# Quarter products with w_in one block earlier, with three moves in the order of the work: a recurrent attention block and an MLP on one Trainium2 core

## The chip, the core and the metric

The kernel runs on one core of a Trainium2 chip. A core has five engines that work through queues of their own and wait for one another by semaphores: TensorE (PE, with its weight loads shown apart as PEld), VectorE (DVE), ScalarE (ACT), GpSimd (POOL) and SyncE (SP), which here only issues DMA transfers. The metric is the time of one execution in microseconds, taken as the median of several.

## The reference

The inputs are q, k, v of 4 batches, 8 heads, 768 time steps and 48 numbers, a beta per step, and two weight matrices. A delta rule runs over time, with a 48 × 48 state per batch and head, and an MLP with a hard-swish follows on its 3072 × 384 output:

```python
for t in range(S):
    kt, vt, bt = k_n[:, :, t], v[:, :, t], beta[:, :, t, None]   # k_n: k over its norm
    y[:, :, t] = einsum('bhd,bhde->bhe', q[:, :, t], state)
    v_old = einsum('bhde,bhd->bhe', state, kt)
    state = state + bt[..., None] * einsum('bhd,bhe->bhde', kt, vt - v_old)
x = y as (3072, 384)
h = x @ w_in                                   # 384 x 2048
out = (h * clip(h + 3, 0, 6) / 6) @ w_out      # 2048 x 384
```

## The kernel before

**Steps and groups.** Time is cut into N = 24 token steps of 32 time steps, each for all four batches at once (4 × 32 = 128 rows). Within a step the recurrence is solved with an inverse of a unit triangular 32 × 32 matrix per head. A step has two halves: `prep(t)`, some steps ahead, which normalizes the keys (kb, L510, on POOL), transposes keys and queries (pt, L524), copies them out of PSUM (KQ, L532, on ACT), forms the scores (sc, L547, 32 small products) and masks them into L and LB (L558, on DVE); and `chain(t)`, which needs the state: products with the state (ks, L806), the right side R (L901, L909, on DVE), its product with the inverse (pz, L827), the update of the state (su, L938; L956), the output (py, L827; y, L819 and L863) and its transposition (yt, L873) into xT (L877). Four steps make a group, whose inverses DVE forms together in some 60 small instructions (L759, L764) between two transpositions (L469, L473). The norms of a group's keys are squares (L409, on POOL), row sums (L413, on DVE) and a few small instructions.

**Blocks of the MLP.** Two steps make one of 12 blocks of 256 tokens. Each block has an up stage (x times w_in, then hard-swish into g) and a down stage (g times w_out). Up comes in two forms. `up` takes sixteen units, each three products of 128 × 256, a relu on ACT (L1001) and a product on DVE (L1004). `up_by_eleven` treats two of the three slices of w_in as 2 × 2 quarters and takes seven products of 128 × 128 and two of 128 × 256 for a pair of units instead of six of 128 × 256. It needs the sums S1, S2, S4 and W21 of quarters of w_in (`weight_sums`, 16 instructions on POOL, L1030) and, for each block, four sums of the tokens (`token_sums`, L1056, on DVE). In it, `begin(j)` issues four products and copies them out (L1080 on ACT, two additions L1030 on POOL); `end(j)` issues the other five and adds (L1093, L1097 on DVE); then come `first` (L1100 and the relu L1104, on ACT) and `rest` (L1107, on DVE). The relu writes into a buffer of the pool name "o", of which there is one, the same in which the down stage's result lies until it is stored. The down stage is `down_by_seven` from block 2 on: 7 products of quarters in 14 units, with additions on DVE and POOL (L1228), copies on ACT (L1225) and, at the end, eight stores (L1143) issued by SP, in the last block by SP and ACT.

**The order.** Everything is issued in an order written by hand; each engine works through its part of it in order. Up to step 4 a list of words (`ORDER`) sets it. From step 5 on a loop does it: each step t has 15 units u; in each unit a table `plan` issues a piece of the chain or of `prep` of a later step, then one unit of the MLP follows, then some instructions of the inverse or the norms (`fill`), as many as a budget (`USED`, `CHAIN`, `mode`) allows. The MLP's unit stands behind the chain's piece in each unit, so products of both alternate on PE. Two steps are 30 units, and a block is 14 + 16 units, so each block meets the same pieces of the chain. Up of block b begins in unit 12 of step 2b + 1, and its remaining units fall to step 2b + 2.

**PSUM.** Two rings of buffers: "pm", four tiles, for most products, and "pc", two tiles of two banks, for ks, sc and su. A product waits until the tile that it takes has been read.

These lines say where the forms change and where the scores of a step are issued:

```python
UF = 5                                    # blocks from UF on: up_by_eleven
...
sums = weight_sums() if blk == UF - 1 else iter(())
...
2: lambda: (take(ch), take(now), take(gens["q"], 4)),   # queries transposed
3: lambda: take(ch),
4: lambda: (take(ch), take(now)),         # chain: pz; prep: scores
5: lambda: take(now),                     # prep: L and LB, then bkb
6: lambda: take(now),
8: lambda: take(ch),                      # chain: su and py
```

Of the kernel before, what the change touches and what calls it, by code (L numbers as in the profile page):

```python
# [44 lines left out]
def kernel(  # L45
# [23 lines left out]
    DM, FF = moe_w_in.shape  # L69
    C, DP = 32, 64  # L70
    P = B * C
    assert P == 128 and S % C == 0 and D <= DP and H % 2 == 0
    N = S // C
# [6 lines left out]
    CB = 2  # L80
# [14 lines left out]
    def rows(b):  # L95
        return slice(C * b, C * b + C)
# [59 lines left out]
    def read(*keys):  # L156
        for key in keys:
            past.add(("read", key))
            reads.setdefault(key, len(reads))
# [53 lines left out]
    for j, value in enumerate((1.0, -1.0)):  # L213
        m = mask2[:, j, :]
        for b in range(B):
            nc.gpsimd.memset(mask2[rows(b), j, :], value)
            nc.gpsimd.affine_select(
                out=mask2[rows(b), j, :], in_=mask2[rows(b), j, :], pattern=[[1, C]],
# [796 lines left out]
                past.add(("up", blk))  # L1015
            yield

    UF = 5
    S1, S2, S4 = (sums_in[:, i] for i in range(3))

    def w_tiles(s, i):
# [37 lines left out]
    def up_by_eleven(blk):  # L1059
        needs(("sums", blk))  # L1060
        B11, T3x, B21, B22, _, _ = x_tiles(blk)
        B3 = xTs[blk][:, 2].rearrange("p (i c) -> p i c", c=P)
        phs, ready = {}, {}

        def mm(ph, n, w, x, start=False, stop=False):
            nc.tensor.matmul(  # L1066
                ph[:, n], lhsT=w, rhs=x, start=start, stop=stop, skip_group_check=True
            )

        def begin(j):  # L1070
            key = ("ph", blk, "by", j)
            ring("pm", NPM, key)
            ph = phs[j] = psM.tile([128, 4, P], FP32, name="ph", tag=slot["pm"])
            mm(ph, 0, W11[:, j], B11, start=True)
            mm(ph, 1, S1[:, j], T1x)
            mm(ph, 2, W21[:, j], T3x)
            mm(ph, 3, S2[:, j], T2x)
            gs[blk, j] = g_all[:, 2 * j : 2 * j + 2]
            gt = gs[blk, j].rearrange("p i (t c) -> p (i t) c", c=P)
            nc.scalar.activation(out=gt, in_=ph[:], func=ACTF.Copy)  # L1080
            plus_minus(gt[:, 3:1:-1], gt[:, 0:2], gt[:, 3:1:-1], ALU.add)
            plus_minus(gt[:, 0], gt[:, 0], gt[:, 2], ALU.add)

        def end(j):
            ph = phs.pop(j)
            mm(ph, 0, W12[:, j], B21)
            mm(ph, 1, S4[:, j], B22)
            mm(ph, 2, W22[:, j], T4x)
            mm(ph, slice(0, 2), W13[:, j], B3)
            mm(ph, slice(2, 4), W23[:, j], B3, stop=True)  # L1090
            g = gs[blk, j].rearrange("p i c -> p (i c)")
            gt = gs[blk, j].rearrange("p i (t c) -> p (i t) c", c=P)
            nc.vector.tensor_tensor(  # L1093
                out=gt[:, 1:3], in0=ph[:, 1:3],
                in1=gt[:, 3].unsqueeze(1).to_broadcast([128, 2, P]), op=ALU.add,
            )
            nc.vector.tensor_tensor(out=gt[:, 3], in0=ph[:, 3], in1=gt[:, 0], op=ALU.add)  # L1097

            def first():
                nc.scalar.activation(out=gt[:, 0], in_=ph[:, 0], func=ACTF.Copy)  # L1100
                read(("ph", blk, "by", j))
                ro = mlp.tile([128, CB, DM], FP32, name="o", bufs=1)
                r = ro[:].rearrange("p c m -> p (c m)")[:, 0 : 2 * TB]
                nc.scalar.activation(out=r, in_=g, func=ACTF.Relu, bias=half, scale=1.0 / 6.0)  # L1104

                def rest():
                    nc.vector.scalar_tensor_tensor(  # L1107
                        out=g, in0=r, scalar=1.0, in1=g, op0=ALU.min, op1=ALU.mult
                    )

                ready[j] = rest

            ready[j] = first
            if j == NPR - 1:
                past.add(("up", blk))

        def go(j):
            if j in ready:
                ready.pop(j)()

        begin(0)
        yield
        begin(1)
        yield
        for j in range(NPR):
            end(j)
            go(j - 1)
            if j + 2 < NPR:
                yield
                begin(j + 2)  # L1130
                go(j)
                yield
            else:
                go(j)
                if j == NPR - 1:
                    go(j)
                yield

    def to_dram(t, o):
        for b in range(B):  # L1140
            r0 = b * S + t * C
            eng = nc.scalar if t >= N - CB and b % 2 else nc.sync
            eng.dma_start(out=out[r0 : r0 + C, :], in_=o[rows(b ^ 1)])  # L1143

    def down(blk, c, f0):

# [32 lines left out]
    HF, HM = NFC // 2, DM // 2  # L1179
# [19 lines left out]
    def down_by_seven(blk):  # L1199
        def A(f, i, j, n=2):  # L1200
            return g_all[:, f + HF * j : f + HF * j + n, i * P : i * P + P]

        def sums(op, out, a, b, f):
            nc.vector.tensor_tensor(out=A(f, *out, 4), in0=A(f, *a, 4), in1=A(f, *b, 4), op=op)  # L1204

        lo, hi, A11, A12, A21, A22 = 0, 4, (0, 0), (0, 1), (1, 0), (1, 1)
        o = mlp.tile([128, CB, DM], FP32, name="o", bufs=1)
        u = mlp.tile([128, HM], FP32, name="u", bufs=1)[:]
        C11, C12, C21, C22 = (o[:, c, m : m + HM] for c in range(CB) for m in (0, HM))
        ps = {}  # L1210

        def product(n, a, b, half):

            if half == 0:
                ring("pm", NPM, ("po", blk, "by", n))
                ps[n] = psM.tile([128, HM], FP32, name="po", tag=slot["pm"])
            for f in range(half * HF // 2, (half + 1) * HF // 2):
                nc.tensor.matmul(  # L1218
                    ps[n][:], lhsT=A(f - f % 2, *a)[:, f % 2], rhs=b[:, f],
                    start=(f == 0), stop=(f == HF - 1),  # L1220
                )

        def copy(out, n, scale=1.0):
            read(("po", blk, "by", n))
            nc.scalar.activation(out=out, in_=ps[n][:], func=ACTF.Copy, scale=scale)  # L1225

        def add(out, a, b, eng=nc.vector):
            eng.tensor_tensor(out=out, in0=a, in1=b, op=ALU.add)  # L1228

        near = nc.gpsimd if blk + 1 < N // CB else nc.vector  # L1230

        settle()
        product(1, A11, B11, 0)
        yield
        product(1, A11, B11, 1)
        copy(u, 1)
        yield
        product(4, A22, T4, 0)
        yield
        product(4, A22, T4, 1)  # L1240
        copy(C21, 4, -1.0)
        sums(ALU.add, A22, A21, A22, lo)
        yield
        product(2, A12, B21, 0)
        sums(ALU.add, A22, A21, A22, hi)
        yield
        product(2, A12, B21, 1)
        copy(C11, 2)
        sums(ALU.subtract, A21, A11, A21, lo)
        yield  # L1250
        product(5, A22, T1, 0)
        sums(ALU.subtract, A21, A11, A21, hi)
        yield
        product(5, A22, T1, 1)
        copy(C22, 5)
        add(C11, C11, u, near)
        sums(ALU.subtract, A11, A22, A11, lo)
        yield
        product(7, A21, B12, 0)
        sums(ALU.subtract, A11, A22, A11, hi)  # L1260
        yield
        product(7, A21, B12, 1)
        copy(C12, 7)
        sums(ALU.subtract, A12, A12, A11, lo)
        yield
        product(6, A11, T2, 0)
        sums(ALU.subtract, A12, A12, A11, hi)
        yield
        product(6, A11, T2, 1)
        yield  # L1270
        product(3, A12, B22, 0)
        add(u, u, ps[6][:])
        read(("po", blk, "by", 6))
        add(C12, C12, u, near)
        add(C21, C21, C12, near)
        yield
        add(u, u, C22, near)
        add(C22, C22, C12, near)
        to_dram(blk * CB + 1, o[:, 1])
        product(3, A12, B22, 1)  # L1280
        add(C12, u, ps[3][:])
        read(("po", blk, "by", 3))
        to_dram(blk * CB, o[:, 0])
        yield

    def mlp_units():
# [43 lines left out]
    def take(gen, n=1):  # L1330
        for _ in range(n):
            while next(gen, None) == 1:
                pass
# [107 lines left out]
    with tc.manual_schedule():  # L1441
# [11 lines left out]
        loads = iter(())  # L1453
        left = due = 0
        USED = {"up": 0.42, "eleven": 1.0, "down": 0.7}
        CHAIN = {0: 0.45, 1: 0.75, 2: 0.75, 3: 0.4, 4: 0.4, 6: 0.5, 9: 0.8, 10: 0.6, 14: 0.2}
        for t in range(LS, N):
            g, i = group(t)
            ch = chain_of(t)
# [8 lines left out]
            if i == 2:  # L1468
# [3 lines left out]
                1: lambda: (take(ch), take(now)),  # L1472
                2: lambda: (take(ch), take(now), take(gens["q"], 4)),
                3: lambda: take(ch),
                4: lambda: (take(ch), take(now)),
                5: lambda: take(now),
                6: lambda: take(now),
                8: lambda: take(ch),
                9: lambda: take(ch),
                10: lambda: take(ch),  # L1480
# [70 lines left out]
```

## Time and profile before

| | |
|---|---|
| median of 3 runs | 666.08 us (665.9 to 666.21) |
| the profiled execution | 669.68 us, its span from first to last instruction 667.9 us |
| granted TensorE clock, mean | 0.98 |
| SP's and ACT's transfers, share of 16 DMA engines' span | 21.1% and 0.2% |

The profile comes from one execution. Its page lists the busy time of each engine, the chain of work that ended last, and groups of like instructions by source line; the trace behind it answers questions on windows, lines and waits. A row of the timeline begins with start and duration in us; behind it, in brackets, stands the time that the engine sat idle before and what ended that. In the chain, "issue" is time in which an engine waited for nothing that the profile shows. PE's records come two for each product of the source, and each has a weight load beside it in PEld.

### The profile page before, as it was taken

The numbers are of one execution on the slowest core, as the hardware profiler recorded it, in microseconds if no ns is written. First come the engines' busy times: TensorE is split into PE (matmuls) and PEld (weight loads), VectorE is DVE, ScalarE is ACT, GpSimd is POOL, SyncE is SP. The second block draws the span as 40 slices with busy tenths as digits, with TensorE's granted clock in tenths as the row PEclk, the third lists the DMA queues.
The fourth block names the chain that finished last, engine by engine and source line by source line (L and its number), as shares of the span: only waits on it lengthen the run. The fifth ranks groups of instructions, "written<-read, shape, count | busy, mean of one in ns | idle before, by whom it ended". The sixth has DMA issues, their size and how long they took to land.

```text
span 667.9 us, 26330 instructions
## 1 busy us (share of the span) xinstructions
PE 636.2 (95%) x11544; PEld 568.0 (85%) x11544; DVE 485.9 (73%) x1146; ACT 272.6 (41%) x532; POOL 203.9 (31%) x320
## 2 busy tenths in 40 slices
PE   2658999999999999999999999999999999999997
PEld 2547987776689988988989989999999999999997
DVE  5879876899545697747988857988748988456353
ACT  5887779432133132232244244245244144153250
POOL 6421032002511130463155255055052241331430
PEclk9767999999999999999999999999999999999999
DMA  7996247302040030031030030020020020010000
GB/s 175 223 240 157 71 97 168 61 13 49 18 89 14 3 73 2 2 79 32 3 68 9 2 67 10 2 62 2 3 50 2 2 49 2 20 21 2 25 1 25
DMA packets 88499, 33.27 MB, mean 50 GB/s; under 512 B 80160, under 2 KB 83232, under 8 KB 88384
## 3 DMA queue, kind: packets, MB, share of 16 engines
q1 hardware_dynamic: 88128, 31.29, 21.1%
q8 instruction: 91, 1.49, 0.9%
q10 hardware_dynamic: 256, 0.30, 0.2%
q14 instruction: 24, 0.20, 0.1%
HBM read 26.84 MB, written 4.72 MB: 47 GB/s over the span
## 4 chain that ended last, share of the span: by engine, by line
PE 88%; DVE 3%; ACT 3%; DMA 2%; issue 2%; SPq 1%; POOL 0%; ACTq 0%; DVEq 0%; POOLq 0%
PE po L1218 28%; PE ph L1066 20%; PE ph L994 15%; PE po L1154 6%; PE ks L806 3%; PE su L938 3%; PE pt L524 3%; PE pz L827 3%; PE py L827 3%; PE sc L547 2%; DMA kf<-in_k_dram 2%; ACT spare L356 2%; PE yt L873 1%; PE pi L684 1%; DVE pr L730 0%
## 5 line engine op out<-in xcount | busy, mean ns | idle before, releaser
L1066 PE MATMUL ph<-xT,w_in 128*128 128x128 f32 (+1 forms) x560 | 121.6, 321 | 0.7 <-issue 0.4
L994 PE MATMUL ph<-xT,w_in 128*128 128x256 f32 (+1 forms) x576 | 117.6, 354 | 1.0 <-ACT xT L877 0.6
L1218 PE MATMUL po<-w_out,g 128*128 128x192 f32 x640 | 110.6, 326 | 0.0
L994 PEld LDWEIGHTS ph<-xT,w_in 128*128 128x128 f32 x576 | 95.6, 195 | 13.8 <-ACT xT L877 1.0
L1218 PEld LDWEIGHTS po<-w_out,g 128*128 128x128 f32 x640 | 104.6, 190 | 0.5
L1066 PEld LDWEIGHTS ph<-xT,w_in 128*128 128x128 f32 x560 | 91.1, 191 | 6.0 <-ACT KQ L532 0.7
L1030 POOL TENSOR_TENSOR g<-g 128x256 f32<-128x256 f32 x112 | 68.0, 609 | 83.4 <-ACT g L1080 79.0
L1218 PE MATMUL po<-spare,g 128*128 128x192 f32 x480 | 86.7, 332 | 0.0
L1218 PEld LDWEIGHTS po<-spare,g 128*128 128x128 f32 x480 | 77.2, 190 | 1.8
L1001 ACT ACTIVATE g<-ph,halves 128x256 f32<-128x256 f32 (+1 forms) x96 | 41.2, 436 | 75.7 <-PE ph L994 75.7
L1228 POOL TENSOR_TENSOR o<-o,u 128x192 f32<-128x192 f32 x18 | 13.2, 733 | 175.7 <-ACT o L1225 97.2
L1080 ACT ACTIVATE g<-ph 128x512 f32<-128x512 f32 x56 | 33.4, 597 | 81.3 <-PE ph L1066 81.3
L1204 DVE TENSOR_TENSOR g<-g 128x512 f32<-128x512 f32 x80 | 55.6, 716 | 5.6 <-PE po L1218 5.6
L759 DVE TENSOR_TENSOR pr<-A 128x30 f32<-128x30 f32 (+9 forms) x150 | 56.8, 379 | 2.7
L764 DVE TENSOR_TENSOR A<-A,pr 128x30 f32<-128x30 f32 (+9 forms) x150 | 55.7, 371 | 3.7
L1004 DVE SCALAR_TENSOR_TENSOR g<-g,ph 128x256 f32<-128x256 f32 (+1 forms) x96 | 34.7, 371 | 29.4 <-ACT g L1001 29.2
L356 ACT ACTIVATE spare<-spare,places 128x768 uint16<-128x768 uint16 (+1 forms) x56 | 52.5, 942 | 2.8 <-DMA kf<-in_k_dram 1.7
L1093 DVE TENSOR_TENSOR g<-ph,g 128x256 f32<-128x256 f32 x56 | 23.5, 420 | 38.5 <-PE ph L1066 33.8
L1225 ACT ACTIVATE o<-po 128x192 f32<-128x192 f32 x40 | 13.2, 330 | 83.2 <-PE po L1218 79.6
L1107 DVE SCALAR_TENSOR_TENSOR g<-o,g 128x512 f32<-128x512 f32 x56 | 40.7, 726 | 6.0 <-ACT o L1104 5.9
L1154 PE MATMUL po<-w_out,g 128*128 128x384 f32 x128 | 45.0, 489 | 0.0
L1104 ACT ACTIVATE o<-g,halves 128x512 f32<-128x512 f32 x56 | 40.5, 722 | 10.1 <-DVE g L1107 5.7
(141 smaller groups left out, 988.1 us busy)
## 6 DMA issues: line engine op xcount, KB each, us to landing
kf<-in_k_dram SPq DMA_DIRECT2D x96, 48.0 KB, 2.9
qb<-in_q_dram SPq DMA_DIRECT2D x96, 48.0 KB, 2.6
vf<-in_v_dram SPq DMA_DIRECT2D x96, 48.0 KB, 2.2
out_dram<-o SPq DMA_DIRECT2D x92, 48.0 KB, 1.6
spare<-in_moe_w_in_dram SPq DMA_DIRECT2D x4, 768.0 KB, 5.8
w_out<-in_moe_w_in_dram SPq DMA_DIRECT2D x4, 768.0 KB, 5.3
w_out<-in_moe_w_out_dram SPq DMA_DIRECT2D x4, 768.0 KB, 6.9
spare<-in_moe_w_out_dram SPq DMA_DIRECT2D x4, 768.0 KB, 5.3
```

The costliest lines, as they stand in the source:

```text
L356: nc.scalar.activation(out=z, in_=z if n else d.bitcast(I16)[:, :, :, 3], func=func, bias=places[:, n : n + 1], scale=scale,)
L759: nc.vector.tensor_tensor(out=pv, in0=A[:, j + 1 :, j].unsqueeze(2).to_broadcast([n, w, j]), in1=A[:, j, 0:j].unsqueeze(1).to_broadcast([n ...
L764: nc.vector.tensor_tensor(out=A[:, j + 1 :, 0:j], in0=A[:, j + 1 :, 0:j], in1=pv, op=ALU.subtract)
L994: nc.tensor.matmul(ph[:, cols], lhsT=w_in[:, s, f * 128 : (f + 1) * 128], rhs=xT[:, s, cols], start=(s == 0), stop=(s == NKT - 1),)
L1001: nc.scalar.activation(out=g, in_=ph, func=ACTF.Relu, bias=half, scale=1.0 / 6.0)
L1030: nc.gpsimd.tensor_tensor(out=out, in0=a, in1=b, op=op)
L1066: nc.tensor.matmul(ph[:, n], lhsT=w, rhs=x, start=start, stop=stop, skip_group_check=True)
L1104: nc.scalar.activation(out=r, in_=g, func=ACTF.Relu, bias=half, scale=1.0 / 6.0)
L1107: nc.vector.scalar_tensor_tensor(out=g, in0=r, scalar=1.0, in1=g, op0=ALU.min, op1=ALU.mult)
L1154: nc.tensor.matmul(pos[c][:], lhsT=gs[blk, f // 2][:, f % 2, c * P : (c + 1) * P], rhs=w_out[:, f, :], start=(f == 0), stop=(f == NFC - 1),)
L1204: nc.vector.tensor_tensor(out=A(f, *out, 4), in0=A(f, *a, 4), in1=A(f, *b, 4), op=op)
L1218: nc.tensor.matmul(ps[n][:], lhsT=A(f - f % 2, *a)[:, f % 2], rhs=b[:, f], start=(f == 0), stop=(f == HF - 1),)
```

## The change

Four edits:

- `UF` is 4 instead of 5: block 4's up is done by `up_by_eleven`, and the sums of w_in's quarters are made during the units of block 3's down stage, not block 4's. The budget of the inverse (`mode`) changes a block earlier with it.
- In `up_by_eleven` of blocks before 9, `first` of pair 0 issues only its copy L1100; the relu follows at the next unit (`second`), and `rest` of pair 0 one unit after that, just ahead of `first` of pair 1.
- For step 12 the scores are issued in unit 6 instead of 4, and L, LB and bkb in unit 7 instead of 5 (`APART`).
- In the last block the first 192 columns of the tile `o[:, 0]` are stored as soon as they are added up, and only the other 192 at the end.

```diff
-    UF = 5
+    UF = 4
...
             def first():
                 nc.scalar.activation(out=gt[:, 0], in_=ph[:, 0], func=ACTF.Copy)
                 read(("ph", blk, "by", j))
+                if j == 0 and blk < 9:
+                    ready[j] = second
+                else:
+                    second()
+
+            def second():
                 ro = mlp.tile([128, CB, DM], FP32, name="o", bufs=1)
                 r = ro[:].rearrange("p c m -> p (c m)")[:, 0 : 2 * TB]
                 nc.scalar.activation(out=r, in_=g, func=ACTF.Relu, bias=half, scale=1.0 / 6.0)
...
                 begin(j + 2)
+                if j == 1:
+                    go(0)
                 go(j)
...
-    def to_dram(t, o):
+    def to_dram(t, o, m=slice(0, DM)):
...
-            eng.dma_start(out=out[r0 : r0 + C, :], in_=o[rows(b ^ 1)])
+            eng.dma_start(out=out[r0 : r0 + C, m], in_=o[rows(b ^ 1), m])
...
         add(C11, C11, u, near)
+        last = blk + 1 == N // CB
+        if last:
+            to_dram(blk * CB, o[:, 0], slice(0, HM))
...
-        to_dram(blk * CB, o[:, 0])
+        to_dram(blk * CB, o[:, 0], slice(HM if last else 0, DM))
...
+        APART = (12,)
...
-                4: lambda: (take(ch), take(now)),
-                5: lambda: take(now),
+                4: lambda: (take(ch), take(now, t not in APART)),
+                5: lambda: take(now, t not in APART),
                 6: lambda: take(now),
+                7: lambda: take(now, t in APART),
```

## The prediction

> **What bounds the kernel now.** I read the page first, then the chain of waits in order of time, then the busy time of the engines block by block. From the page (span, busy times, the queue that brings instructions, the chain by engine):
>
> ```profile
> span 667.9 us, 26330 instructions
> ...
> PE 636.2 (95%) x11544; PEld 568.0 (85%) x11544; DVE 485.9 (73%) x1146; ACT 272.6 (41%) x532; POOL 203.9 (31%) x320
> ...
> q8 instruction: 91, 1.49, 0.9%
> ...
> PE 88%; DVE 3%; ACT 3%; DMA 2%; issue 2%; SPq 1%; POOL 0%; ACTq 0%; DVEq 0%; POOLq 0%
> ```
>
> TensorE is busy for 95% of the span and holds 88% of the chain. The windows below run from one boundary of the chain to the next and hold the up stages of blocks 3, 4, 5, 6 and 7. Columns: us; busy time and instructions of PE, PEld, DVE, ACT, POOL; granted clock; DMA.
>
> ```profile
> 233.76:260.59 26.83, 26.83 (x429) 23.03 (x429) 23.79 (x60) 9.56 (x20) 6.54 (x9) 1.00 0.22 46
> ...
> 284.89:311.72 26.83, 26.83 (x429) 23.04 (x428) 16.36 (x40) 9.56 (x20) 15.46 (x23) 1.00 0.35 69
> ...
> 336.03:362.28 26.25, 25.96 (x478) 23.44 (x477) 22.38 (x52) 12.81 (x26) 14.32 (x23) 1.00 0.23 48
> 386.58:412.90 26.32, 25.90 (x477) 23.59 (x476) 16.26 (x39) 12.93 (x26) 13.52 (x23) 1.00 0.23 48
> 437.21:463.16 25.95, 25.95 (x478) 23.44 (x477) 22.50 (x52) 12.93 (x26) 14.57 (x23) 1.00 0.20 41
> ```
>
> In blocks 3, 4 and 7 PE is as busy as the window is long; what such a stage is worth is PE's own time in it. Blocks 5 and 6 have holes of 0.29 and 0.42 us. The chain shows where they lie:
>
> ```profile
> 311.72 2.60 PE po L1218 x16
> ...
> 339.58 2.80 DMA out_dram<-o
> ...
> 343.02 0.72 ACT o L1104
> 343.74 0.49 ACT KQ L532
> ...
> 344.27 2.69 PE ph L1066 x18
> ...
> 397.14 0.81 PE pz L827 x64
> 397.95 0.79 PE sc L547 x53
> ...
> 399.94 0.42 issue
> ```
>
> In block 5 (from 336.03) the chain leaves PE: the eight stores of block 4's tile land at 342.38, the first relu (L1104) writes the same buffer and starts at 343.02, the copy of the transposed keys (KQ) stands behind it on ACT, and PE's next product waits for the PSUM tile that this copy frees. In block 6 PE stops for 0.42 us with nothing that the profile could name as awaited, just behind pz and sc. So a gain must come from PE's work or from these two holes.
>
> **The change part by part.** The sum is made against the profiled execution, 669.68 us with a span of 667.9; the median of the runs is 666.08, 3.6 us less, and I apply the difference to the median.
>
> 1. Block 4's up by quarter products. Plain up of blocks 3 and 4 takes 26.83 us each, with one token step's chain and one preparation beside it; the quarter products of block 7, with the same chain and preparation (478 − 144 = 334 other instructions against 429 − 96 = 333), take 25.95 without a hole. 26.83 − 25.95 = 0.88 us saved on PE. ACT, DVE and POOL get more to do in this stage: in block 7 DVE was busy 22.50 and POOL 14.57 of 25.95, and PE had no hole, so I take nothing. The four sums of tokens that DVE makes for such a block stand at the end of block 3's down, as block 5's did at the end of block 4's; the chain goes from that down into up on PE. Term: −0.88.
>
> 2. The 16 weight sums on POOL move a block earlier. By the order of instructions, 14 now stand in POOL's queue behind the kb product of 236.97 and run in up of block 3; two follow the addition that opens POOL's tail of the down stage.
>
> ```profile
> 236.36 0.89 DVE L764 TENSOR_TENSOR A<-A,pr 128x210 f32<-128x210 f32 x1
> 237.17 0.41 DVE L1004 SCALAR_TENSOR_TENSOR g<-g,ph 128x256 f32<-128x256 f32 x1
> ...
> 239.27 0.40 DVE L764 TENSOR_TENSOR A<-A,pr 128x228 f32<-128x228 f32 x1
> ...
> 264.22 0.74 DVE L901 SCALAR_TENSOR_TENSOR R<-ks,parity,vf 128x192 f32<-128x192 f32 x2 [0.96 <-PE ks L806]
> 265.80 0.69 DVE L1204 TENSOR_TENSOR g<-g 128x512 f32<-128x512 f32 x1 [0.84 <-PE po L1218]
> ...
> 267.83 1.99 DVE L473 STREAM_TRANSPOSE X<-A 128x1024 f32<-128x1024 f32 x1
> ...
> 236.97 0.96 POOL L510 TENSOR_TENSOR kb<-kf,inv 128x384 f32<-128x384 f32 x1
> ...
> 288.44 0.72 POOL L1030 TENSOR_TENSOR sums_in<-w_in 128x256 f32<-128x256 f32 x1
> ...
> 322.67 1.17 POOL L1030 TENSOR_TENSOR sums_in<-w_in,sums_in 128x256 f32<-128x256 f32 x1
> 323.81 0.86 POOL L1030 TENSOR_TENSOR w_in<-w_in 128x256 f32<-128x256 f32 x1
> ...
> 270.54 0.81 PE pz L827 x64
> ```
>
> Up of block 3 is the stage in which DVE has least room: 23.79 busy of 26.83, since the inverse of a group ends there. The row for two engines at once is L764: 0.89 us with POOL working beside it, 0.40 for a larger tile with POOL idle, so up to 0.49 lost to a POOL instruction; L1004, which reads PSUM, keeps 0.41 under the same POOL instruction. Upper bound 14 × 0.49 = 6.9 us of DVE time, lower bound 0. DVE's room before PE feels it: 26.83 − 23.79 = 3.04 idle, then 0.96 + 0.84 of waits for PE in the down stage, and the transposed inverse is ready at 267.83 + 1.99 = 269.82 for pz at 270.54, another 0.72: 5.56 in all. About half of DVE's instructions there are L759 and L764, so I take some 3.5 us, the middle of the bounds: all inside the room. Term: 0, bounds 0 and +1.3.
>
> The Trainium skill, "GPSIMD Engine Reference", section Specifications, says that POOL shares its SBUF interfaces with VectorE and that they contend when a VectorE instruction has two SBUF inputs. The trace agrees in kind (0.89 against 0.41). Read as full exclusion it is the slower rival below.
>
> 3. The last two sums now stand in front of the squares of the keys (L409), whose sums (L413) DVE awaits in turn.
>
> ```profile
> 271.99 1.27 POOL L409 TENSOR_TENSOR sq<-kf 128x384 f32<-128x384 f32 x1
> ...
> 279.36 0.55 DVE L413 TENSOR_REDUCE ss<-sq 128x8 f32<-128x384 f32 x1 [0.72 <-POOL sq L409]
> 279.83 0.55 DVE L863 TENSOR_TENSOR y<-y,py 128x384 f32<-128x384 f32 x1
> ...
> 281.96 0.33 PE yt L873 x3
> ```
>
> The two took 1.17 + 0.86 = 2.03 us, so the squares, DVE's four L413 and y's addition (L863, ends 280.38) move by up to 2.03, to 282.41. PE takes the transposition of y at 281.96: a wait between 0 and 0.45. DVE was busy when the first square was ready, which swallows part of the shift; I take 0.1. Behind y stand the state update, u's addition and the sums of tokens that open block 4's up; they have the same slack. Term: +0.1.
>
> 4. The relu of a block's first pair, blocks 4 to 8, a unit later. KQ's copy then goes ahead of it on ACT, the stores should have landed by then, and block 5 loses its hole: 26.25 − 25.95 = 0.30; I count the 0.29 of PE. What is late next: relu of the second pair uses the same buffer and waits for DVE's L1107 of the first, which now comes a unit later. Both are 0.7 us pieces (the row 452.78 below is the slow case) on engines that are not full; bounds −0.29 and 0. In block 4 this shift is what covers the stores, which there start as late as in block 5. Term: −0.29.
>
> 5. Step 12's scores (sc, 32 small products) two units later. Instructions reach PE in packets: 2 × 11544 / 91 = 254 each. Counting PE's instructions in both programs, pz of block 6 stands at place 83 of a packet of 256, and there pz and sc, 256 instructions in 1.6 us, were followed by the hole. The quarter products add 100 instructions to block 4, so in block 6 the place becomes 183, which block 3 had before without a hole; place 79 falls to step 12 in block 5, where pz and sc are now parted. So I expect the hole of 0.42 to go: −0.42, bounds −0.42 and 0. The cost: the step issues no DMA, but DVE's L558 and POOL's bkb move with it, past a pair's additions and POOL's two; su needs the PSUM tile that L558 frees.
>
> ```profile
> 449.38 5.05 PE ph L1066 x36
> ...
> 448.96 0.41 DVE L1093 TENSOR_TENSOR g<-ph,g 128x256 f32<-128x256 f32 x1
> ...
> 451.24 0.41 DVE L558 TENSOR_TENSOR LB<-sc,mb 128x256 f32<-128x256 f32 x1
> ...
> 452.78 1.00 DVE L1107 SCALAR_TENSOR_TENSOR g<-o,g 128x512 f32<-128x512 f32 x1
> ```
>
> Before, 36 records (5.05 us) lay between sc and su; now 18, 2.5 us. DVE needs, from a pair's L1093 to the second L558, 451.24 + 0.41 − 448.96 = 2.69 us, and one more inverse instruction (0.4) stands in between; L1093 can start 0.8 us, sc's duration, before sc ends. 3.1 against 3.3: just enough, and L1107 at 1.00 beside POOL takes 0.3 more. Bounds 0 and 0.5; I take 0.15. Terms: −0.42 and +0.15.
>
> 6. The last tile in halves. Four more DMAs, two on SP and two on ACT, are issued in the eighth of the last stage's fourteen units; ACT's next copy comes two units later (16 records, 2.60), and SP has nothing.
>
> ```profile
> 663.33 1.93 ACTq L1143 DMA_DIRECT2D out_dram<-o  x4
> 664.02 0.35 DVE L1228 TENSOR_TENSOR o<-u,po 128x192 f32<-128x192 f32 x1 [0.73 <-PE po L1218]
> ...
> out_dram<-o SPq DMA_DIRECT2D x92, 48.0 KB, 1.6
> ```
>
> At the end the same eight issues remain: four on each queue in 1.93 us, the last of them after DVE's last addition. Only the final four carry half the bytes. A landing of 48 KB takes 1.6 us; if it were all bytes, half of it, 0.8, would go; if it were all latency, nothing. The issues (1.93 for four of 48 KB) are spaced alike whether SP or ACT makes them, so I take the lower end: −0.05, bounds −0.8 and 0.
>
> Sum: −0.88 + 0.1 − 0.29 − 0.42 + 0.15 − 0.05 = −1.39, that is 666.08 − 1.39 = 664.7 us, −0.21%.
>
> **The rivals.**
> - The hole stays, or another packet boundary makes one, so that moving sc gains nothing: −1.39 + 0.42 = −0.97, 665.1. For it: only one hole in the trace to learn from. Against it: of the ten pz directly ahead of sc in blocks 3 to 7, only the one at place 83 had a hole.
> - The relu's shift does nothing, since ACT waits for the stores all the same or for L1107: −1.39 + 0.29 = −1.1, 665.0.
> - The squares come late and PE waits for y: with 0.45 there and as much again at the sums of tokens, −0.6, 665.5.
> - Better than the sum: neither of the two small waits arises and the tail's half lands 0.3 sooner: −1.39 − 0.25 − 0.3 = −1.9, 664.1.
> - The slower one: POOL and DVE exclude each other fully. Then each of the 14 sums costs DVE its 0.72, 10.1 in all, less the room of 5.56: PE waits 4.5 for the inverse or for y, −1.39 + 4.5 = +3.1, 669.2. Against it: DVE read PSUM unhindered under POOL, and waited at most 0.49. The change turns to a loss from (1.39 + 5.56) / 14 = 0.50 per sum, and passes +0.2% at (1.39 + 1.33 + 5.56) / 14 = 0.59.
>
> **How the numbers follow.** 0.2% of 666.08 is 1.33 us, about what a measurement of this kernel can tell from no change. The forecast lies on that bound: its own range, 664.3 to 665.0, is worth 0.45, three quarters of it under 664.75. The better case gets 0.14, the hole 0.14, the relu 0.08, the late squares 0.12, the slower one 0.07. Faster: 0.34 + 0.14 = 0.48; within 0.2%: 0.11 + 0.14 + 0.08 + 0.12 = 0.45; slower 0.07. The range, 663.9 to 665.6, leaves out the slower rival and the ends of the others.
>
> **What would show it.** Right: up of block 4 near 26.0 us with PE busy throughout; no DMA in the chain of block 5; no hole above 0.1 us behind pz; PE without a wait at yt (near 282) and at su of step 12. Wrong: DVE over 26 us busy in up of block 3, PE waiting for L473 or L863 there, KQ's copy still behind L1104, or a hole at another pz. Most likely wrong: PE's waits in the new block 4, for which only blocks 5 to 7 stand as a model.

## The result, and the profile after

The changed kernel takes 664.29 us in the median against 666.21 for the kernel before on the same chip (19 runs each): a ratio of 0.9968, interval 0.9958 to 0.9978, that is 2.1 us less (1.5 to 2.8). The forecast was 664.7, 1.39 us less: the right sign, a time inside the range, and a gain a third too small.

From the page of the changed kernel, span and chain by engine:

```profile
span 660.6 us, 26484 instructions
...
PE 92%; ACT 3%; DVE 2%; DMA 2%; SPq 1%; issue 0%; ACTq 0%; DVEq 0%
```

One execution's span differs from the next by some 5 us, since block 2's up begins anywhere between 175.7 and 180.7 us after the start. Behind it, stages in which PE has no wait, shown or hidden, repeat to 0.03 us. So the runs below are compared stage by stage too. The table is worked out from the traces: us from the first product of a stage to the first of the next, the tail (from the end of DVE's last addition to the end of the span), and the whole from block 2's up to the end of the span. The stages that it leaves out are alike to 0.03 us in all these runs.

```
              before  after    e1     e2     e3     e4     e6     e7     e8     e9    e10
up block 3     26.83  27.09  27.09  26.83  27.10  26.83  28.64  26.83  27.73  26.83  27.10
down block 3   24.31  24.42  24.41  24.31  24.43  24.31  25.37  25.16  29.69  24.31  24.42
up block 4     26.83  25.58  26.08  26.83  25.58  26.83  25.58  25.58  25.58  25.58  25.58
up block 5     26.25  25.78  25.76  25.70  27.18  25.98  25.77  25.77  25.78  25.77  25.78
up block 6     26.32  25.69  25.58  25.58  25.58  26.01  25.68  25.67  25.58  25.68  25.69
down block 6   24.31  24.31  24.38  24.31  24.58  24.31  24.31  24.31  24.31  24.42  24.76
up block 7     25.95  25.85  26.41  25.77  25.92  25.77  25.91  25.81  26.00  25.80  25.94
tail            3.48   3.00   3.39   3.51   2.99   3.02   3.08   2.99   2.99   3.00   2.90
whole         487.22 484.68 486.04 485.78 486.31 486.03 487.29 485.06 490.59 484.35 485.12
```

Between the two profiled executions some 2.5 us went: +0.26 and +0.11 in block 3, −1.25, −0.47, −0.63 and −0.10 in the ups of blocks 4 to 7, −0.48 in the tail. The windows of the same stages in the changed kernel (columns as in the prediction):

```profile
229.02:256.11 27.09, 27.08 (x428) 22.91 (x428) 26.31 (x58) 9.67 (x20) 17.50 (x23) 1.00 0.22 45
256.11:280.54 24.43, 24.43 (x446) 23.19 (x445) 19.18 (x44) 5.09 (x12) 9.57 (x10) 1.00 0.01 3
280.54:306.12 25.58, 25.58 (x477) 23.48 (x477) 16.57 (x40) 12.93 (x26) 14.05 (x24) 1.00 0.37 72
330.43:356.20 25.77, 25.77 (x476) 23.40 (x476) 21.62 (x52) 12.82 (x26) 14.50 (x23) 1.00 0.23 49
```

In up of block 3 POOL is now busy 17.50 instead of 6.54 us and DVE 26.31 instead of 23.79. Block 4 takes 25.58, less than blocks 5 to 7 did before. The chain says why: from the changed kernel, in order of time (start, duration, what).

```profile
251.68 0.55 PE yt L873 x3
...
277.49 0.44 PE yt L873 x3
...
288.49 2.43 PE ph L1066 x18
...
301.83 0.33 PE yt L873 x3
...
340.81 0.81 PE pz L827 x64
341.62 2.62 PE ph L1066 x18
344.25 0.79 PE sc L547 x53
345.04 2.62 PE ph L1066 x18
...
351.91 0.33 PE yt L873 x3
```

The same pieces in the kernel before, in blocks 6 and 7:

```profile
394.54 2.60 PE ph L1066 x18
...
445.17 2.62 PE ph L1066 x18
...
458.69 0.51 PE yt L873 x3
```

The eighteen records ahead of pz take 2.43 us now and took 2.62, 2.60 and 2.69 in blocks 7, 6 and 5. A transposition of y (yt) takes 0.33 when y is there, and 0.51 in block 7 before. So the "busy" PE of block 7, the model for block 4, held 0.19 + 0.18 us of waiting: with the later relu alone (e2) that block takes 0.18 less. In block 3 the same reading shows the price: yt takes 0.55 in up and 0.44 in down, where it took 0.33 before.

### The profile page after: what moved, and what is told of

Read it like the earlier page. It is cut to its first block, busy times and chain, and to the rows that moved or that the text cites. A ratio compares the mean times of both kernels' runs of the same rounds, so it can differ in the third digit from the quotient of the medians.

```text
span 660.6 us, 26484 instructions
## 1 busy us (share of the span) xinstructions
PE 633.3 (96%) x11592; PEld 567.8 (86%) x11592; DVE 492.7 (75%) x1158; ACT 276.7 (42%) x540; POOL 217.0 (33%) x336
## 4 chain that ended last, share of the span: by engine, by line
PE 92%; ACT 3%; DVE 2%; DMA 2%; SPq 1%; issue 0%; ACTq 0%; DVEq 0%
PE po L1226 28%; PE ph L1066 24%; PE ph L994 12%; PE po L1162 6%; PE ks L806 4%; PE pt L524 3%; PE py L827 3%; PE pz L827 3%; PE sc L547 3%; PE su L938 3%; ACT spare L356 2%; DMA kf<-in_k_dram 1%; PE yt L873 1%; PE pi L684 1%; DVE pr L730 1%; DVE A L735 0%
## 5 line engine op out<-in xcount | busy, mean ns | idle before, releaser
L1066 PE MATMUL ph<-xT,w_in 128*128 128x128 f32 (+1 forms) x640 | 139.0, 321 | 0.0
L1066 PEld LDWEIGHTS ph<-xT,w_in 128*128 128x128 f32 x640 | 104.0, 191 | 5.9
L1030 POOL TENSOR_TENSOR g<-g 128x256 f32<-128x256 f32 (+1 forms) x128 | 78.3, 613 | 92.8 <-ACT g L1080 87.8
L994 PE MATMUL ph<-xT,w_in 128*128 128x256 f32 (+1 forms) x480 | 93.3, 343 | 1.5 <-DVE g L1004 1.0
L994 PEld LDWEIGHTS ph<-xT,w_in 128*128 128x128 f32 x480 | 76.2, 190 | 11.5 <-DVE g L1004 1.3
L1080 ACT ACTIVATE g<-ph 128x512 f32<-128x512 f32 x64 | 38.2, 597 | 92.8 <-PE ph L1066 92.8
L759 DVE TENSOR_TENSOR pr<-A 128x30 f32<-128x30 f32 (+9 forms) x150 | 58.8, 392 | 3.1
L764 DVE TENSOR_TENSOR A<-A,pr 128x30 f32<-128x30 f32 (+9 forms) x150 | 56.0, 373 | 3.5
L1001 ACT ACTIVATE g<-ph,halves 128x256 f32<-128x256 f32 (+1 forms) x80 | 33.7, 428 | 56.7 <-PE ph L994 56.7
L1113 DVE SCALAR_TENSOR_TENSOR g<-o,g 128x512 f32<-128x512 f32 x64 | 46.4, 725 | 6.8 <-ACT o L1110 6.8
L1110 ACT ACTIVATE o<-g,halves 128x512 f32<-128x512 f32 x64 | 46.2, 723 | 10.5 <-DVE g L1113 7.8
L1066 PE MATMUL ph<-beta_tok,sums_in 128*128 128x128 f32 x256 | 49.5, 275 | 0.0
L510 POOL TENSOR_TENSOR kb<-kf,inv 128x384 f32<-128x384 f32 x24 | 21.7, 905 | 74.0 <-issue 43.1
```

The lines of the kernel that those rows point to most:

```text
L759: nc.vector.tensor_tensor(out=pv, in0=A[:, j + 1 :, j].unsqueeze(2).to_broadcast([n, w, j]), in1=A[:, j, 0:j].unsqueeze(1).to_broadcast([n ...
L764: nc.vector.tensor_tensor(out=A[:, j + 1 :, 0:j], in0=A[:, j + 1 :, 0:j], in1=pv, op=ALU.subtract)
L994: nc.tensor.matmul(ph[:, cols], lhsT=w_in[:, s, f * 128 : (f + 1) * 128], rhs=xT[:, s, cols], start=(s == 0), stop=(s == NKT - 1),)
L1030: nc.gpsimd.tensor_tensor(out=out, in0=a, in1=b, op=op)
L1066: nc.tensor.matmul(ph[:, n], lhsT=w, rhs=x, start=start, stop=stop, skip_group_check=True)
L1113: nc.vector.scalar_tensor_tensor(out=g, in0=r, scalar=1.0, in1=g, op0=ALU.min, op1=ALU.mult)
```

## The experiments

### The parts alone: e1, e2, e4

**e1: quarter products from block 4, nothing else.**

```diff
-    UF = 5
+    UF = 4
```

> Block 4's up as quarter products alone; the relu, step 12's scores and the tail as before. My theory, after the changed kernel's trace: up of block 3 pays about 0.25 us (y late, 27.1 against 26.83) and its down 0.13 (24.43 against 24.30) for the sums of w_in on POOL; up of block 4 takes 25.6 + 0.2 + 0.3 = 26.1, since its first relu stands behind the stores as block 5's did. The hole of 0.42 leaves block 6; if it hangs on the place of pz and sc in PE's instructions (place 79 of 256 now falls to step 12 of block 5), block 5 gets one of 0.3 to 0.5 behind pz and sc and the sum is -0.3 (665.9 us). Rival: the hole hangs on something else of step 14 (its loads, DVE's order): then it stays in block 6, at 0.4, and block 5 has only its 0.29 at ph. Rival of the prediction for block 4: 25.95 with no wait.

Measured: ratio 1.0006 (0.9986 to 1.0027), no gain; whole 486.04. Block 3 pays the 0.26 and 0.10. Block 4 comes to 26.08, with its first relu behind the stores as foreseen, and block 7, which had no such hole before, gets one:

```profile
PE ph L1066 <- ACT KQ L532: 0.5, 2, 0.2
```

```profile
434.28 2.79 DMA out_dram<-o
...
437.64 0.72 ACT o L1104
438.36 0.49 ACT KQ L532
...
438.90 2.69 PE ph L1066 x18
```

The stores of the block before land at 434.28 + 2.79 = 437.07, L1104 follows, KQ's copy behind it, and PE waits. Block 5, which had this hole in the profile of before, had none here. Which block pays hangs on when the stores land in that execution; the hole is not block 5's own. And block 5 has no stop behind pz and sc, although its instructions stand where I had put the risk: taken alone this speaks against the place.

**e2: the later relu, nothing else** (the `second` of the change's diff, and `go(0)` at j == 1).

> The later relu alone. My theory: it takes KQ's copy from behind L1104 in every block 5 to 7, so up of block 5 goes from 26.25 to 25.77, of block 6 by 0.19 (18 records ahead of pz in 2.43 instead of 2.60), of block 7 by 0.1 to 0.2; block 6 keeps its hole; sum -0.8, 665.4 us. As predicted: only block 5 gains, 0.29, and 6 and 7 nothing. Rival: nothing at all, since ACT waits for the stores anyhow.

Measured: ratio 0.9972 (0.9958 to 0.9987), whole 1.44 us less: −0.55, −0.74 and −0.18 in blocks 5 to 7. Block 6's part holds the 0.42 of its hole, which did not occur in this execution; that is a miss of the expectation, taken up below. Without it 1.02 remains. The relu moves KQ's copy ahead in blocks 5 to 7, not only where a hole was seen, as I had expected after the trace and not in the prediction. By the times this part alone, 0.9972, can't be told from the whole change, 0.9968, while e1 and e4 can't be told from no change.

**e4: the last tile in halves, nothing else** (`to_dram` with `m`, and `last`).

> The last tile in halves alone. Predicted -0.05. From the changed kernel's trace: from the end of DVE's last addition to the end of the span 3.00 us instead of 3.49, so -0.3 to -0.5, 665.8 us, and everything before the last stage as before. Rival: the 0.5 is chance of that one execution, and 3.4 to 3.5 is seen here.

Measured: the tail 3.02, as in the changed kernel (3.00); 48 KB stores gave 3.39 to 3.51 in five traces, 24 KB stores 2.99 to 3.08 in eight. So some 0.4 us is real. The time itself, ratio 1.0001 (0.9985 to 1.0017), can't tell it from nothing. In this execution block 5's first relu waited 0.36 us instead of 0.64, and PE had no hole there. In blocks 6 and 7 KQ's copy was in time without the later relu (2.43 us for the eighteen records), so what the relu saves differs from execution to execution as well. Block 6's stop is there again, 0.28 us long.

### The stop behind pz and sc: e3, e5, e11, e12

**e3: the changed kernel with step 12's scores back in unit 4.**

```diff
-        APART = (12,)
+        APART = ()
```

> The changed kernel with step 12's scores back in unit 4. If the hole hangs on the place in PE's instructions, one of 0.3 to 0.5 us appears in up of block 5 within 2 us behind pz and sc (window 26.1 to 26.3 against 25.77), +0.4 us in all; block 6 has none. If the place is not the reason, block 5 stays at 25.7 to 25.8 and the time is that of the changed kernel.

Measured: ratio 0.9986 (0.9969 to 1.0004), whose interval overlaps that of the changed kernel, so by the times alone parting is not shown to gain. In the trace up of block 5 is 27.18, 1.40 longer and more than expected, and PE stops in the middle of sc:

```profile
343.38 0.81 PE pz L827 x64
344.20 0.69 PE sc L547 x47
344.88 1.19 issue
346.07 0.33 PE sc L547 x11
```

sc's 32 products read one tile and write one tile; a wait for another engine would have held the first of them, not the last. That leaves the supply of instructions. The trace records each packet that brings them to PE (16 KB). Worked out from it, with PE's instructions numbered in the program's order (four for each product, two for a transposition, one for any other; in the prediction I had counted four for transpositions too):

```
run, stage        pz begins  packet from, to   PE stops at   resumes  after landing
before, up 6        397.14   397.89  398.77       15042      400.35      1.58
e4, up 6            394.30   394.71  395.96       15042      397.37      1.41
e2, up 6            395.38   395.01  396.60       none
e3, up 5            343.38   343.67  344.55       13250      346.07      1.52
e1, up 5            341.09   339.36  340.34       none
```

The same order of instructions stops at the very same place, 15042, in two executions, and not in the third, where the packet set out before pz did. e3 and e1 share an order too, and only e3 stopped. The stop ends 1.4 to 1.6 us after the packet has landed.

**e5: the kernel before with each sc of steps 14 to 23 issued twice.**

```diff
+                    for _ in range(2 if t >= 14 else 1):
                         nc.tensor.matmul(scv[rows(b), e, p], ...)
```

> The kernel before with every sc of steps 14 to 23 issued twice into the same tile: 0.79 us more PE work in each of ten steps, from block 3 on, and a run of 384 instead of 256 small instructions behind each pz. If the holes of 0.28, 0.42 and 1.19 us are PE running out of instructions (each ended 1.4 to 1.6 us after an instruction packet had landed), there are more and longer ones now: stops of PE of 0.3 to 1.5 us within 2 us of pz in at least four of the ten steps, each ending 1.4 to 1.6 us behind a landing; sum +7.9 for the work and +2 to +8 for the stops. Rival: the holes are waits for another engine (DVE's reads of sc) or one that the place of the step sets: then +0.79 in each stage with a second sc, and at most the hole of block 6.

Measured: ratio 1.0326 (1.0288 to 1.0364), 25.3 us from block 2 to the end, of which 10 × 0.79 is the work. Waits of PE, and one of the stops in the chain:

```profile
PE sc L548 <- issue: 9.9, 7, 1.9
```

```profile
355.31 0.81 PE pz L828 x64
356.12 1.45 PE sc L548 x87
357.57 1.92 issue
359.49 0.48 PE sc L548 x22
```

Seven of ten steps stop, for 0.98 to 1.92 us, 9.9 in all (more than the 2 to 8 expected), each until 1.24 to 1.52 us after a landing. Two more waits are KQ's (0.69 and 2.33 us). Behind the longer of them the granted clock was 0.50 for 3.4 us, which accounts for up to 1.7 (half of 3.4); some 2.8 was not traced further. The seven stand at the instructions 9666, 10690, 11714, 12738, 13762, 14786 and 15810: exactly four times 256 apart. And 15042 and 13250 above, 9666 in e8, 13762 in e11 and 16066 in e10 all leave the same remainder, 194, when divided by 256; so does 9922, where a stop of 0.24 us in e6 stands, in py behind su. PE's waits for KQ's copy leave others (44, 77, 117, 199). The count also gives the number of packets: 23272 / 256 = 90.9 for the kernel before, where the page says 91, and 24552 / 256 = 95.9 here, where it says 96. So PE runs dry at the end of a packet. In this run the end lies 275 to 364 instructions behind the start of pz in the seven steps that stop, and 180, 214 and 241 in the three that don't.

**e11: as many small products more in the kernel before, but spread** (twos, fours and fives ahead of the products of up and down in the same ten stages).

```diff
+            for _ in range(4 if blk < 8 else 0):
+                nc.tensor.matmul(ph[0:32, 0, 0:64], lhsT=W11[0:64, j, 0:32], rhs=B11[0:64, 0:64], ...)
             mm(ph, 0, W11[:, j], B11, start=True)
```

> The kernel before with 320 small products more, as many as in the run with sc twice, in the same ten stages, but in twos to fives ahead of the products of up and down. If that run lost 20 us because 384 small instructions in a row outrun the packets, this one shows none of its stops: no wait without a cause above 0.5 us in blocks 3 to 7 beyond the one of block 6, and each stage 0.8 to 2.5 us longer (32 products of 0.025 us and the changes of tile size). If the number of instructions is what costs, the stops of 0.7 to 2.3 us are here too, up of block 5 at 29 and more.

Measured: the stops are gone but for one:

```profile
PE ph L1071 <- issue: 0.3, 1, 0.3
```

So it is the run of small instructions that empties the supply, not their number. My size for the price was far off: the ratio is 1.0834 (1.0802 to 1.0867), 4.5 to 7.8 us a stage, 54.6 in all or 0.17 for each of the 320 products. Two small products between large ones hold PE for 262.83 − 262.49 = 0.34 us, where 32 in a row take 0.79:

```profile
262.49 0.41 PE L994 MATMUL ph<-xT,w_in 64*32 64x64 f32 x4
262.83 0.70 PE L999 MATMUL ph<-xT,w_in 128*128 128x256 f32 x2
```

They differ in two ways, the change of tile (64 × 32 against 128 × 128) and that all of them use one part of the array; which of them costs was not tried.

**e12: step 15's scores parted too**, on the version e9 (told below). In the changed order of PE's instructions a packet ends 269 behind pz of step 15, in block 6's down; e10's stop of 0.29 stands there (16066 = 15797 + 269). The same stage is longer in e1, e3 and e9, without a stop that the trace shows as one. In the seven traces with this order the packet set out 0.2 to 0.4 us behind the start of pz; how long the stage takes follows the packet's landing:

```
                                    e6     e7  after     e1     e9     e3    e10
packet lands, us behind pz's start  1.18   1.24   1.30   1.33   1.34   1.52   1.59
down of block 6                    24.31  24.31  24.31  24.38  24.42  24.58  24.76
```

```diff
-        APART = (12,)
+        APART = (12, 15)
```

> The version with S1, S2 and S4 a block earlier and W21 first, and step 15's scores parted from pz as step 12's are. By PE's instructions numbered with two for a transposition and four for any other product, each stop of PE without a releaser so far stands at place 194 of 256, and in the unchanged order of the steps the end of a packet falls 235 to 339 instructions behind the start of pz where there were stops; in the changed kernel that is step 12 (235, parted) and step 15 in block 6's down (269, not parted), whose stage took 24.31, 24.31, 24.31, 24.38, 24.42, 24.58 and 24.76 in seven traces of that order. Theory: with step 15 parted no stage of blocks 3 to 7 has a wait without a cause, block 6's down takes 24.31 to 24.5 (one more change between large and small products, 0.19), and from block 2 to the end it takes 484.2 to 484.5. If the place has nothing to do with it, the stop appears in block 6's down or at another step all the same, 0.1 to 1 us.

Measured: no wait without a cause in the profiled execution, but block 6's down takes 24.81, and the whole 484.82:

```profile
419.34 2.80 PE po L1230 x16
422.14 0.79 PE sc L547 x53
422.93 2.80 PE po L1230 x16
425.73 0.25 PE su L938 x4
...
426.01 0.84 PE su L938 x46
```

Two pieces of 2.80 for one of 5.40 cost 0.20, and su, now only one piece behind sc, begins and stands still: 0.25 + 0.03 + 0.84 for 0.82. So here the delay costs what it did not cost in block 5. The timed runs went further: 665.2 to 671.6, ratio 1.0015 (0.9995 to 1.0035), so that this version gave back the gain. The profiled execution, at 665.21 one of its two shortest, does not show what the longer ones lose; that stays open.

### The sums of w_in beside DVE: e6, e7, e9

**e6: the changed kernel with S1, S2 and S4 each computed twice** (`for _ in range(2)` around each of the three).

> The changed kernel with S1, S2 and S4 each computed twice, 12 more sums on POOL. If the +0.26 us in up of block 3 is DVE slowed by POOL (L764 0.7 to 0.8 instead of 0.4, so y late for PE), the sums now run to the end of the stage and into down: up of block 3 27.2 to 27.8, down 24.5 to 25.2. If POOL's sums delay nothing but the squares behind them, up of block 3 stays at 27.09 and only down grows.

Measured: up of block 3 is 28.64, more than expected, down 25.37; ratio to the kernel before 1.0001 (0.9983 to 1.002), so all of the gain is gone. The waits of PE there:

```profile
PE yt L873 <- DVE y L863: 1.4, 2, 0.9
PE pz L827 <- DVE R L909: 0.5, 1, 0.5
```

Twelve sums cost (28.64 − 27.09) + (25.37 − 24.42) = 2.50 us, 0.21 each, once DVE's room is used up. How a sum costs, in the timeline of the changed kernel: DVE's rows up to y, the sum beside them on POOL, and PE's weight load for yt, which waited 0.41 us for y.

```profile
248.72 0.80 DVE L764 TENSOR_TENSOR A<-A,pr 128x220 f32<-128x220 f32 x1
249.44 0.41 DVE L1004 SCALAR_TENSOR_TENSOR g<-g,ph 128x256 f32<-128x256 f32 x1
249.77 0.57 DVE L759 TENSOR_TENSOR pr<-A 128x210 f32<-128x210 f32 x1
250.37 0.79 DVE L764 TENSOR_TENSOR A<-A,pr 128x210 f32<-128x210 f32 x1
251.08 0.54 DVE L863 TENSOR_TENSOR y<-y,py 128x384 f32<-128x384 f32 x1
...
250.07 0.86 POOL L1030 TENSOR_TENSOR w_in<-w_in 128x256 f32<-128x256 f32 x1
...
251.68 0.20 PEld L873 LDWEIGHTS yt<-ident,y 128*128 128x128 f32 x2 [0.41 <-DVE y L863]
```

The same L764 on 220 columns took 0.39 in the kernel before, with POOL idle; L1004, which reads PSUM, keeps 0.41. The Trainium skill, "GPSIMD Engine Reference", section Specifications, names contention with VectorE instructions of two SBUF inputs; the trace agrees, and gives the size: 0.4 us for such an instruction, not the whole 0.86 of POOL's.

**e7: the sums a block earlier, those into W21 (`last_sums`) late in block 3's down.**

```diff
-            sums = weight_sums() if blk == UF - 1 else iter(())
-            for _ in downs(blk):
-                next(sums, None)
-                next(sums, None)
+            sums = weight_sums() if blk == UF - 2 else last_sums() if blk == UF - 1 else iter(())
+            for n, _ in enumerate(downs(blk)):
+                if blk < UF - 1 or n > 6:
+                    next(sums, None)
+                    next(sums, None)
```

> The changed kernel with S1, S2 and S4 issued a block earlier (in the units of block 2's down; POOL runs ahead into up of block 2, where DVE was busy 13.6 of 28.6 us), and the four sums into W21 in the second half of block 3's down. My theory: up of block 3 back to 26.83, its down 24.31 to 24.42, blocks 4 and on as in the changed kernel: -0.3 us against it, 663.9. Rival: DVE is slowed as much in block 2's up and down, and the 0.26 comes up there; or the late W21 hold up block 4's first products.

Measured: ratio 0.9976 (0.996 to 0.9992). Up of block 3 is back at 26.83, so the 0.26 was POOL's. But down takes 25.16, since two of W21's four sums now stand ahead of the first square (L409) in POOL's queue and two ahead of the second, the squares come late to L413, and y behind it late to PE:

```profile
PE yt L873 <- DVE y L863: 0.7, 1, 0.7
```

This is the mechanism of the prediction's third step, and four sums among the squares cost more than the two of the change did (0.85 against 0.11).

**e9: the same, with W21's sums at the start of block 3's down** (no `n > 6`).

> S1, S2 and S4 a block earlier as before, but the four sums into W21 at the start of block 3's down, so that POOL does them ahead of its additions and squares. If the 0.73 that block 3's down lost last time came from W21's sums standing ahead of the squares, and four sums are few enough for y in up of block 3 (L863 ended 1.8 us ahead of its need there before the change, and twelve sums took 2.2), then up of block 3 is 26.83 to 26.95 and down 24.31; from block 3's up to the end 0.35 us less than the changed kernel, 0.33% under the kernel before it, or 664.2 us by its median of the first comparison. Rival: W21's sums wait for PE in up of block 3 and hold up POOL's masks and bkb behind them: up of block 3 above 27.1.

Measured: ratio 0.9959 (0.9943 to 0.9975). Both stages of block 3 are as before the change:

```profile
233.62:260.45 26.83, 26.83 (x429) 23.03 (x428) 23.39 (x59) 9.58 (x20) 7.42 (x11) 1.00 0.24 46
260.45:284.76 24.31, 24.31 (x446) 23.24 (x445) 19.61 (x43) 5.11 (x12) 10.20 (x12) 1.00 0.01 3
```

From block 2 to the end it takes 484.35, 0.33 less than the changed kernel, though 0.11 of block 6's down is against it here. This is the best version found; by the times it can't be told from the changed kernel, since the intervals of the ratios overlap.

### Block 3 by quarter products: e8

```diff
-    UF = 4
+    UF = 3
```

> The changed kernel with UF = 3: block 3's up by quarter products too, the sums of w_in beside block 2. My theory: up of block 3 goes from 27.09 to 25.6 and its down from 24.42 to 24.31, since POOL's sums fall into block 2, where DVE has room; -1.5 us, 662.7. Rival: DVE, 23.8 busy of 26.83 there before with one instruction a product, gets some 5 us more (L1093, L1097, L1107 in place of L1004) and cannot finish: PE waits 1 to 3 us for it, and nothing is gained.

Measured: ratio 1.0019 (1.0002 to 1.0036), whole 490.59, 5.91 more than the changed kernel. The rival was right: DVE can't finish the inverse beside the quarter products' additions.

```profile
PE pz L827 <- DVE X L473: 2.5, 1, 2.5
PE ph L1066 <- issue: 0.9, 1, 0.9
PE yt L873 <- DVE y L863: 0.8, 1, 0.8
```

PE waits 0.9 us for instructions and 0.8 for y in up of block 3, and 2.5 for the transposed inverse (L473) in its down. The rest of down's loss is not waiting. Behind the wait of 2.5 us the same pieces take up to twice as long, and the row of that window shows why, a granted clock of 0.50 (third column from the end):

```profile
273.06 1.50 PE pz L827 x64
...
275.68 7.26 PE po L1226 x32
```

```profile
272.70:279.30 6.60, 6.24 (x140) 5.98 (x141) 5.35 (x12) 0.49 (x1) 1.20 (x1) 0.50 0.01 2
```

Elsewhere pz takes 0.81, sc 0.79 and these 32 records 5.40; here they took 1.50, 1.11 and 7.26, 2.87 more. 24.31 + 2.50 + 2.87 = 29.68, the 29.69 of down of block 3.

### The tail: e10

```diff
-        to_dram(blk * CB, o[:, 0], slice(HM if last else 0, DM))
+        to_dram(blk * CB, o[:, 0], slice(HM, HM + 16) if last else slice(0, DM))
```

> The changed kernel, with the last four stores cut to 16 of their 192 columns; the other 176 columns of these 128 rows are not stored, so this part of the output is missing. It separates bytes from the rest of a store's time in the tail (from DVE's last addition to the end of the span: 3.48 us with 48 KB stores, 3.00 with 24 KB). If bytes set the tail, 24 KB less gave 0.48 and the 22 KB that go now give 0.3 to 0.5 more: 2.5 to 2.7. If it is issue and latency, as I took it in the prediction, it stays at 2.95 to 3.05.

Measured, in one execution: 2.90. From 48 to 24 KB the tail lost some 0.4, from 24 to 2 KB 0.1, little more than the tails with 24 KB differ among themselves (2.99 to 3.08). The last addition and the span, of this run:

```profile
span 664.0 us, 26484 instructions
```

```profile
660.71 0.35 DVE L1236 TENSOR_TENSOR o<-u,po 128x192 f32<-128x192 f32 x1 [0.73 <-PE po L1226]
```

664.0 − 661.06 = 2.9. So neither theory holds as put: bytes count between 48 and 24 KB and hardly below. Why the first half weighs so much was not tried.

## Why the prediction was right, and where its sum was wrong

- **Bound.** Right: PE's own time in a stage and two holes. But I took "as busy as the window is long" for work. PE's rows hold waits of 0.1 to 0.2 us without showing them as idle.
- **Step 1, block 4 as block 7: −0.88.** The model held 0.37 us of such waits (2.62 for 2.43, 0.51 for 0.33); with the later relu the stage measured −1.25. Alone block 4's up gave −0.75, and with what block 3 pays and the waits behind the stores the time showed nothing (e1). That the relu's shift covers the stores in block 4 was right.
- **Step 2, the sums on POOL: 0, at most +1.3.** Measured +0.26. My estimate of DVE's loss, 3.5 us, was near: L759 and L764 in that stage took 18.4 us for 32 instructions, and 15.4 for 34 before. The room was wrong: I followed only the inverse to the end of the group, and y, in the same queue of the same stage, had 1.8 us (L863 ended at 254.59 before, yt began at 256.37), not 5.56. So two of the signs named for being wrong came true here: DVE was busy for 26.31 us, and PE waited for L863. The slower rival, full exclusion at 0.72 a sum, which would have turned the change to a loss from 0.50 on, is refuted by 0.21 (e6).
- **Step 3, the squares: +0.1.** Right, +0.11, by the mechanism named (yt 0.44 for 0.33); e7 shows it larger.
- **Step 4, the relu: −0.29.** The mechanism was right, the size too small: KQ's copy stood behind L1104 in blocks 6 and 7 too. Alone it is worth about 1.0 us between the traces of before and e2, and by e2's times 1.9 (0.9 to 2.8), more than any other part. How much it saves depends on when the stores land: e4, without it, lost less in the same blocks. The rival that it does nothing fell.
- **Step 5, the hole: −0.42, and +0.15 for the delay.** That PE stops at the end of an instruction packet, and that pz and sc in a row bring it there, is shown. My places were not right: with transpositions counted as two, pz of step 14 stood at 175 and of step 12 at 215, not at 83 and 79; what they share is a packet's end 275 and 235 behind pz. And the place is half of it: it says where PE can stop, the time at which the packet lands says whether it does, and how long. The same order stopped for 0.42, 0.28 and 0 us, the unparted scores of block 5 for 1.19 and 0. So the 0.42 belonged to the profiled execution, not to every run, and the change moved the risk to block 6's down as well, which I had not looked for. The delay cost nothing: parting gives two pieces of 2.62 for one of 5.05 (+0.19) and y is in time for it (0.33 for 0.51); 25.78 against 25.76 unparted (e1).
- **Step 6, the tail: −0.05.** Some −0.4: by ratio the term that was most mis-sized (in us it was step 4's). I took all of a landing for latency; I had named −0.8 as the other end.
- **The rivals.** Nearest came "better than the sum" (664.1), with its tail; the waits at yt that it ruled out did occur.
- **Luck.** That the time lies inside the range owes something to luck. Steps 1, 4 and 6 were too small by about 0.4, 0.7 and 0.4 us; against that stood 0.26 that step 2 had put at nothing, and a hole of 0.42 counted in full that not every execution has.

The Trainium skill, "Runtime: NRT & Kernel Launch", section Instruction fetch mechanics, says that instructions are fetched in blocks of 16 KiB (256 instructions), and that the cost of crossing a block's end is mostly hidden. The first agrees (stops at one place of 256); the second does not hold here: stops of 0.24 to 1.92 us in runs of small products, of which 256 instructions took 1.6 us.

## What to carry to other kernels

Before a stage is taken as the model for another, compare its pieces with the shortest like piece of the trace: an engine at 100% can still be waiting. For a load moved to another engine, look for the nearest reader in the shared queue, not for the last one. Where PE issues hundreds of instructions of small products in a row, it can empty its instruction supply; large products between two such runs can prevent that, but check what the parting costs at the next wait (e12). And count a long wait of PE for more than its length where the granted clock falls behind it (e8).

## What the runs showed of the hardware that was not expected

PE's supply: a stop ends 1.24 to 1.58 us after a packet's landing. With a packet's end 268 to 270 instructions behind the start of pz, a landing up to 1.30 us behind pz cost nothing, one at 1.34 cost 0.11 and one at 1.59 cost 0.45.

The clock: around the end of PE's waits of 2.50 us (e8) and 2.33 us (e5) the granted clock fell to 0.50, for 6.8 and 3.4 us. Otherwise it was 1.00 from block 2 to PE's last product in all fourteen traces, with stops of up to 1.92 us among them. From what length on a wait brings the clock down, and whether it always does, is open.

Small products spread between large ones cost 0.14 to 0.24 us each by the stages of e11, against 0.025 in a row. The Trainium skill, "TensorEngine Tiling (Array Packing)", section Key Properties, says that changing the tiling mode drains TensorE; that fits, but these runs do not separate it from the shared part of the array.
